# A planned attention and gated feed-forward kernel: other due times and other engines for its small jobs

## The chip, the core and the metric

The kernel runs on one core of a Trainium2 chip. TensorE (PE in the profile) multiplies matrices into PSUM; VectorE (DVE), ScalarE (ACT) and GpSimd (POOL) work on tiles in SBUF, and DVE and ACT on PSUM as well; SyncE (SP) issues the DMA transfers. The metric is the device time of one execution in microseconds (us); less is better.

## The reference

Eight batches of eight heads, 576 positions, 64 numbers a head. Queries and keys are rotated (rotary embedding), each head does a softmax attention, the heads of a batch are laid side by side to a 576x512 matrix `x`, and a gated feed-forward follows: a causal convolution of five taps gives the gate, and one matrix each stands before and after the gating.

```python
def rotate(x):
    x1, x2 = (x[..., :half], x[..., half:])
    return np.concatenate([x1 * cos - x2 * sin, x1 * sin + x2 * cos], axis=-1)
q_rot, k_rot = (rotate(q), rotate(k))
scores = scale * np.matmul(q_rot, k_rot.transpose(0, 1, 3, 2))
scores = scores - np.max(scores, axis=-1, keepdims=True)
attn = np.exp(scores)
attn = attn / (np.sum(attn, axis=-1, keepdims=True) + 1e-09)
x = np.matmul(attn, v)
...
for k in range(K):
    gate_pre += conv_w[k][None, None, :] * xp[:, k:k + S, :]
gate = 1.0 / (1.0 + np.exp(-gate_pre))
val = x @ w_val
return (gate * val @ w_out).astype(np.float32)
```

## The kernel before

Two heads make a pair, so there are 32 pairs, `p` = 0 to 31, and four pairs make a batch. The work is cut into 3445 jobs, most of them one instruction on one engine. For a pair they are:

- **Rotary steps**, for `k` and for `q`: two products with the tables (`rope_mul`, L212; keys `kmul0`, `kmul1`, `qmul0`, `qmul1`), their sum (`rope_add`, L216; `kadd`, `qadd`), a rounded high part on ACT (`qk_hi`, L223; `khi`, `qhi`) and the rest as a low part (`qk_lo`, L227; `klo`, `qlo`). `kadd` needs `kmul0` and `kmul1`; `klo` needs `khi`, which needs `kadd`.
- **Scores** on PE (`s_mm`, L255: five groups `s0` to `s4` a pair), the row maximum on DVE (`s_max`, L261), the exponential on ACT (`s_exp`, L274).
- **Turning the probabilities**: in pairs 5 to 30 four block transposes on DVE (`turn`, L289; `x1` to `x7`) and 16 moves by DMA (L294); in pairs 0 to 4 and in pair 31 by PE (L303, L316) with copies out of PSUM on ACT (L190) or DVE (L192), keys `c0` to `c7`.
- **Attention times values** on PE (`pv_last` L359, `pv_mm` L369 to L377), scaled on DVE into `x` (`x_norm`, L405; `norm0`, `norm1`). The sums of the softmax come by `chm`, a small copy on ACT (L190), and a trip through DRAM.
- **Gate**: tap 0 on ACT (L426), taps 1 to 4 on DVE (`tap`, L429), tanh on ACT (L433). `x_hi` (ACT, L412) and `x_lo` (POOL, L416; `xlo`) split `x` for the products.
- **Feed-forward**, for each batch 16 groups of 12 matmuls on PE (`f_mm`, L463): eight of the first stage (`f00` to `f07`), each followed by `y_mul` (DVE, L468), `y_hi` (ACT, L472) and `y_lo` (mostly POOL, L476), and eight of the second (`f10` to `f17`), each followed by a copy out and a DMA.

During pairs 0 to 4 DVE also decodes both weight matrices and the taps (L497 to L504).

What sets the order is `Plan`. Every job has a due time: a base that stands in the code, in a frame of 18.5 us a pair, plus an entry of the table `DUE`. `Plan.order` puts the jobs on one list: always the one with the smallest due time among those whose inputs and buffers are there. Each engine does its own jobs in the order of that list. `PICK` says for some jobs on which engine they go: `V` (DVE), `A` (ACT), `G` (POOL), `SP`. An entry without a suffix holds for pairs 5 to 31, with `e` for pairs 0 to 4 (rotary steps: 1 to 4), with `_0` and `_1` for the two halves of pair 0, with `l` for the last batch or pair.

DVE instructions that read two tensors of SBUF are marked as `port` jobs (rotary steps, taps 1 to 4, some decode steps). A POOL job that stands behind such a DVE job on the list is made to wait for the last one before it; nothing makes a DVE job wait for POOL:

```python
if jobs[i][6] and jobs[i][1] == "V":
    last = i
elif jobs[i][1] == "G" and last is not None:
    self.behind[i] = last
```

Of the kernel before, what the change touches and what calls it, by code (L numbers as in the profile page):

```python
# [35 lines left out]
PICK = {'c0': 'A', 'c0e': 'A', 'c1': 'V', 'c1e': 'V', 'c2': 'V', 'c2e': 'A', 'c3': 'A', 'c3e': 'A', 'c4': 'V', 'c4e': 'A', 'c5': 'A', 'c5e': 'A', 'c6': 'A', 'c6e': 'V', 'c7': 'V', 'c7e': 'A', 'ch0': 'A', 'ch0e': 'V', 'ch1': 'V', 'ch1e': 'A', 'chm': 'A', 'chme': 'A', 'cm': 'A', 'cme': 'A', 'kadd': 'G', 'kadd_0': 'V', 'kadd_1': 'V', 'kadde': 'V', 'kfront': 'A', 'kfronte': 'A', 'klo': 'G', 'klo_0': 'V', 'klo_1': 'V', 'kloe': 'G', 'kmul0': 'G', 'kmul0_0': 'V', 'kmul0_1': 'V', 'kmul0e': 'G', 'kmul1': 'V', 'kmul1_0': 'V', 'kmul1_1': 'V', 'kmul1e': 'V', 'od0': 'A', 'od0l': 'A', 'od1': 'A', 'od1l': 'V', 'od2': 'A', 'od2l': 'V', 'od3': 'A', 'od3l': 'A', 'qadd': 'G', 'qadd_0': 'V', 'qadd_1': 'V', 'qadde': 'V', 'qlo': 'G', 'qlo_0': 'G', 'qlo_1': 'G', 'qloe': 'G', 'qmixed': 'A', 'qmixede': 'A', 'qmul0': 'G', 'qmul0_0': 'V', 'qmul0_1': 'V', 'qmul0e': 'V', 'qmul1': 'G', 'qmul1_0': 'V', 'qmul1_1': 'V', 'qmul1e': 'V', 'xlo': 'G', 'xloe': 'G', 'xlol0': 'V', 'xlol1': 'G', 'ylo': 'G', 'ylol': 'V', 'ch3': 'V', 'ch3e': 'A', 'decout': 'A', 'decval': 'A', 'odma': 'SP', 'odmal': 'SP', 'loadk': 'SP', 'loadk_0': 'SP', 'loadk_1': 'SP', 'loadke': 'SP', 'loadq': 'SP', 'loadq_0': 'SP', 'loadq_1': 'SP', 'loadqe': 'SP', 'loadv': 'SP', 'loadve': 'SP', 'mv0': 'SP', 'mv1': 'SP', 'mv2': 'SP', 'mv3': 'SP', 'rr': 'SP', 'rre': 'SP', 'rw': 'SP', 'rwe': 'SP'}


class Plan:
# [769 lines left out]
```

## Time and profile before

| | |
|---|---|
| Median of 3 runs | 655.0 us (651.52 to 658.75) |
| The profiled execution | 652.48 us, span 650.7 us |
| DVE busy | 579.1 us (89%), 827 instructions |
| PE busy | 616.9 us (95%), 5683 matmuls |
| PE loading weights | 503.4 us (77%) |
| ACT busy | 462.7 us (71%), 1161 instructions |
| POOL busy | 390.3 us (60%), 297 instructions |
| Granted PE clock, mean | 0.996 |

A share over the whole span mixes three stretches: the head (pairs 0 to 4 with the weights), the steady stretch (pairs 6 to 30, in which a batch of four pairs repeats) and the tail (the last pair and the last batch's products). An instruction on DVE or POOL that waits for the SBUF port is counted as busy: its duration grows. So for these two, durations of equal instructions are compared with each other. The matmuls of PE overlap, so PE's busy share is read beside the time from the first of a group to the first of the next.

### The profile page before, as it was taken

What the parts mean: (1) busy time and instruction counts of PE and PEld (TensorE: products, weight loads), DVE (VectorE), ACT (ScalarE), POOL (GpSimd) and SP (SyncE); (2) the same over time, 40 slices, a digit from 0 to 9 for tenths busy, and PEclk for the clock granted to TensorE, in tenths of its full rate; (3) what the DMA queues carried; (4) which work ended last, traced back from release to release, by engine and by line L of the source; (5) the groups of instructions that cost most, each with busy time, mean ns of one, the idle gap of its engine ahead of it and who ended that gap; (6) DMA issues with size and microseconds to landing.
All of it is one profiled execution on the core that took longest, in us unless ns stands there. A gap on an engine that the chain in (4) does not pass through costs nothing.

```text
span 650.7 us, 15423 instructions
## 1 busy us (share of the span) xinstructions
PE 616.9 (95%) x5683; PEld 503.4 (77%) x5683; DVE 579.1 (89%) x827; ACT 462.7 (71%) x1161; POOL 390.3 (60%) x297
## 2 busy tenths in 40 slices
PE   8899988989899998999999999999999999999997
PEld 7666665678677886888778787888788877788797
DVE  6898999998899999999999999999999999995453
ACT  4788888867777777767877777767777777664521
POOL 1322446776777868687677868766976867630200
PEclk9899999999999999999999999999999999999999
DMA  5524432378989989999999999989999898864102
GB/s 185 225 78 153 162 117 101 114 206 242 268 235 260 258 250 250 263 241 252 239 249 252 241 262 255 267 241 256 254 263 254 233 252 210 249 166 132 56 2 74
DMA packets 51482, 134.43 MB, mean 207 GB/s; under 512 B 10928, under 2 KB 20944, under 8 KB 51408
## 3 DMA queue, kind: packets, MB, share of 16 engines
q1 hardware_dynamic: 50864, 132.86, 72.8%
q8 instruction: 45, 0.74, 0.5%
q10 hardware_dynamic: 544, 0.59, 0.3%
q14 instruction: 29, 0.24, 0.1%
HBM read 62.48 MB, written 9.59 MB: 111 GB/s over the span
## 4 chain that ended last, share of the span: by engine, by line
PE 49%; DVE 23%; DMA 9%; ACT 6%; issue 4%; POOL 4%; SPq 3%; ACTq 0%; DVEq 0%; POOLq 0%
PE ps_t L463 17%; PE ps_t L369 12%; PE ps_s L255 10%; DVE nm L261 8%; DVE big L289 7%; DMA big<-big 5%; DVE g L429 3%; SPq L294 3%; ACT p L274 3%; PE ps_t L359 3%; PE ps_t L303 2%; PE ps_t L374 2%; PE ps_t L330 1%; ACT big L190 1%; DVE g L468 1%
## 5 line engine op out<-in xcount | busy, mean ns | idle before, releaser
L261 DVE TENSOR_REDUCE nm<-ps_s 128x1 f32<-128x576 f32 x288 | 201.8, 741 | 19.9 <-PE ps_s L255 18.8
L274 ACT ACTIVATE p<-ps_s,nm 128x576 f32<-128x576 f32 x256 | 187.7, 738 | 39.5 <-DVE nm L261 38.4
L255 PE MATMUL ps_s<-k,q 64*128 64x288 f32 x1536 | 145.0, 310 | 11.4 <-ACT p L274 9.2
L255 PEld LDWEIGHTS ps_s<-k,q 64*128 64x128 f32 x1536 | 111.0, 184 | 37.6 <-ACT p L274 18.2
L289 DVE STREAM_TRANSPOSE big<-p 128x1152 f32<-128x1152 f32 x104 | 139.8, 1357 | 0.0
L429 DVE SCALAR_TENSOR_TENSOR g<-x,cw,g 128x576 f32<-128x576 f32 (+1 forms) x132 | 122.4, 927 | 0.9 <-ACT g L426 0.6
L369 PE MATMUL ps_t<-big,v 128*64 128x256 f32 (+2 forms) x1024 | 118.4, 382 | 0.0
L227 POOL TENSOR_TENSOR q<-iq,q 128x576 fp32r<-128x576 f32 (+2 forms) x33 | 48.8, 1477 | 94.9 <-ACT q L223 89.8
L369 PEld LDWEIGHTS ps_t<-big,v 128*64 128x64 f32 x1024 | 70.1, 137 | 44.1 <-issue 13.5
L212 POOL TENSOR_TENSOR iq<-iq,tab 128x576 f32<-128x576 f32 x54 | 77.1, 1450 | 19.8 <-DMA iq<-in_q 13.3
L463 PE MATMUL ps_t<-yh,wout_hi 128*128 128x288 f32 x256 | 79.2, 310 | 0.0
L463 PE MATMUL ps_t<-xh,wval_hi 128*128 128x288 f32 x256 | 79.0, 309 | 0.0
L463 PE MATMUL ps_t<-yl,wout_hi 128*128 128x288 f32 x256 | 76.2, 298 | 1.9 <-POOL yl L476 1.9
L463 PE MATMUL ps_t<-xl,wval_hi 128*128 128x288 f32 x256 | 76.3, 298 | 0.0
L463 PE MATMUL ps_t<-xh,wval_lo 128*128 128x288 f32 x256 | 75.9, 297 | 0.0
L463 PE MATMUL ps_t<-yh,wout_lo 128*128 128x288 f32 x256 | 75.5, 295 | 0.0
L227 POOL TENSOR_TENSOR k<-ik,k 128x576 fp32r<-128x576 f32 x31 | 52.5, 1694 | 37.4 <-DVE iq L212 25.0
L476 POOL TENSOR_TENSOR yl<-g,yh 128x288 fp32r<-128x288 f32 x56 | 46.7, 841 | 43.5 <-ACT yh L472 41.2
L416 POOL TENSOR_TENSOR xl<-x,xh 128x576 fp32r<-128x576 f32 (+1 forms) x32 | 47.6, 1487 | 25.5 <-PE ps_t L463 13.4
L463 PEld LDWEIGHTS ps_t<-xh,wval_hi 128*128 128x128 f32 x256 | 48.7, 190 | 2.8 <-issue 1.6
L472 ACT CAST yh<-g 128x288 fp32r<-128x288 f32 x64 | 26.6, 431 | 33.9 <-DVE g L468 33.9
L463 PEld LDWEIGHTS ps_t<-yl,wout_hi 128*128 128x128 f32 x256 | 48.3, 189 | 3.1 <-POOL yl L476 3.0
(95 smaller groups left out, 1107.9 us busy)
## 6 DMA issues: line engine op xcount, KB each, us to landing
big<-big SPq DMA_DIRECT2D x416, 144.0 KB
ik<-in_k SPq DMA_DIRECT2D x31, 576.0 KB
iq<-in_q SPq DMA_DIRECT2D x31, 576.0 KB
v<-in_v SPq DMA_DIRECT2D x32, 320.0 KB
rb<-rd SPq DMA_DIRECT2D x64, 144.0 KB
out_t<-oo SPq DMA_DIRECT2D x64, 144.0 KB
big<-in_w_val SPq DMA_DIRECT2D x4, 512.0 KB
big<-in_w_out SPq DMA_DIRECT2D x4, 512.0 KB
```

Of the source, the lines that this page charges most:

```text
L212: eng.tensor_tensor(out=t[:, i, a:b], in0=t[:, i, a:b], in1=tabs[:, i, a:b], op=ALU.mult)
L227: eng.tensor_tensor(out=t[:, 1], in0=state[p][n + "in"][:, 0, a:b], in1=t[:, 0].bitcast(F32), op=ALU.subtract)
L255: T.matmul(out=ps[:, half, 0:288], lhsT=st["q"][rows, x, c * 128:c * 128 + 128] if c < 4 else mixq[p % 2][:, x], rhs=st["k"][rows, y, k0:k ...
L261: V.tensor_reduce(out=st[f"nm{i}"], in_=st[f"s{i}"], axis=AX.XY, op=ALU.max, negate=True)
L274: A.activation(out=pd.rearrange("p (b x) -> p b x", b=2), in_=st[f"s{i}"], func=AF.Exp, bias=st[f"nm{i}"], scale=1.0, accum_out=sums[p % 2 ...
L289: V.transpose(out=t[:, :, cs.index(c)].rearrange("p b k i -> p k b i"), in_=st[f"p{c}"].rearrange("p h s -> p (h s)").rearrange("p (k b i) ...
L369: T.matmul(out=acc[HEAD[h], 0:n], lhsT=st["v"][:, j, h, :], rhs=st["pt"][:, :, c0:c1, 5 * place(p, 2 * c0 + h) + j].rearrange("p a c i -> ...
L416: eng.tensor_tensor(out=st["xl"][:, a:b], in0=xs[p % 2][:, 4 + a:4 + b], in1=st["xh"][:, a:b].bitcast(F32), op=ALU.subtract)
L429: V.scalar_tensor_tensor(out=g, in0=x_sb[:, a + k:b + k], scalar=w, in1=g, op0=ALU.mult, op1=ALU.add)
L463: T.matmul(out=acc[:, 0:n], lhsT=wt[w][:, kc, ds], rhs=mv, start=(kc == 0 and i == 0), stop=(kc == NCH - 1 and i == 2))
L472: A.copy(out=ffn[b, "h", dc, lo], in_=ffn[b, "y", dc, lo])
L476: eng.tensor_tensor(out=ffn[b, "l", dc, lo], in0=y, in1=ffn[b, "h", dc, lo].bitcast(F32), op=ALU.subtract)
```

## The change

Only the two tables differ, `DUE` and `PICK`. Not one job is added or taken away, and the code that makes the instructions is the same. All entries of `DUE` have new numbers; of those of `PICK` these have another engine:

```diff
-PICK = {'c0': 'A', 'c0e': 'A', 'c1': 'V', 'c1e': 'V', 'c2': 'V',
+PICK = {'c0': 'V', 'c0e': 'V', 'c1': 'A', 'c1e': 'A', 'c2': 'V',
...
-'c3': 'A', 'c4': 'V', 'c4e': 'A', 'c5': 'A', 'c6': 'A', 'c6e': 'V', 'c7': 'V',
+'c3': 'V', 'c4': 'A', 'c4e': 'V', 'c5': 'V', 'c6': 'V', 'c6e': 'A', 'c7': 'A',
...
-'ch1': 'V', 'kadd_1': 'V', 'qadd_1': 'V', 'qmul1_0': 'V', 'qmul1_1': 'V',
+'ch1': 'A', 'kadd_1': 'G', 'qadd_1': 'G', 'qmul1_0': 'G', 'qmul1_1': 'G',
...
-'kmul0e': 'G', 'kmul1e': 'V', 'qmul0e': 'V', 'qmul1e': 'V',
+'kmul0e': 'V', 'kmul1e': 'G', 'qmul0e': 'V', 'qmul1e': 'G',
...
-'od0l': 'A', 'od2l': 'V', 'xlol1': 'G',
+'od0l': 'V', 'od2l': 'A', 'xlol1': 'V',
```

In pairs 5 to 30 no job has another engine; there the change is one of order alone. DVE has seven jobs fewer (814 for 821), POOL seven more.

**On POOL, pairs 14 and 15** (the steady stretch; `iq`, `ik` are the rotary buffers, `yl` the low parts of the feed-forward). Before, from `qadd` of pair 15 on:

```order
L216 TENSOR_TENSOR iq_3544<-iq_3544 128x576
L227 TENSOR_TENSOR q_72<-iq_3544,q_72 128x576
L216 TENSOR_TENSOR ik_3412<-ik_3412 128x576
L212 TENSOR_TENSOR ik_3655<-ik_3655,tab 128x576
L227 TENSOR_TENSOR k_70<-ik_3412,k_70 128x576
L476 TENSOR_TENSOR yl_3851<-g_2768,yh_3850 128x288
```

And now:

```order
L216 TENSOR_TENSOR iq_3515<-iq_3515 128x576
L216 TENSOR_TENSOR ik_3377<-ik_3377 128x576
L227 TENSOR_TENSOR q_72<-iq_3515,q_72 128x576
L212 TENSOR_TENSOR ik_3621<-ik_3621,tab 128x576
L227 TENSOR_TENSOR k_70<-ik_3377,k_70 128x576
L476 TENSOR_TENSOR yl_3850<-g_2753,yh_3849 128x288
```

`kadd` (L216 on `ik`) stands ahead of `qlo` (L227 on `q`) instead of behind it. On the list it and `qlo` now come behind `kmul1` of DVE, which stands between taps 3 and 4; before, `qlo` came ahead of tap 3.

**On ACT at the same place**, from the exponentials of group `s1` on; before:

```order
L274 ACTIVATE p_3843,sums_86<-ps_s_3816,nm_3841 128x576
L274 ACTIVATE p_3843,sums_86<-ps_s_3817,nm_3845 128x576
L223 CAST k_70<-ik_3412 128x576
L190 COPY pq_3834<-ps_t_3886 128x512
L274 ACTIVATE p_3910,sums_86<-ps_s_3871,nm_3908 128x576
```

And now:

```order
L274 ACTIVATE p_3835,sums_86<-ps_s_3819,nm_3833 128x576
L274 ACTIVATE p_3835,sums_86<-ps_s_3820,nm_3837 128x576
L190 COPY pq_3840<-ps_t_3841 128x128
L223 CAST k_70<-ik_3377 128x576
L472 CAST yh_3849<-g_2753 128x288
```

The small copy `chm` (L190, 128x128) comes between the exponentials and `khi` (L223 on `k`), on which `klo` of POOL waits; before it stood ahead of the exponentials.

**On DVE in the head**, pair 3 coming up while pair 2 is scored (`ik_449` and `ik_498`, `iq_627`: rotary buffers; `big`: weights being decoded). Before, from `kmul1` on:

```order
L212 TENSOR_TENSOR ik_449<-ik_449,tab 128x576
L261 TENSOR_REDUCE nm_734<-ps_s_692 128x1
L503 TENSOR_SCALAR big_274<-big_274 128x512
L261 TENSOR_REDUCE nm_752<-ps_s_693 128x1
L429 SCALAR_TENSOR_TENSOR g_579<-x_84,cw,g_579 128x576
L216 TENSOR_TENSOR ik_449<-ik_449 128x576
L504 SCALAR_TENSOR_TENSOR wval_lo<-big_274 128x512
L212 TENSOR_TENSOR iq_627<-iq_627,tab 128x576
L429 SCALAR_TENSOR_TENSOR g_579<-x_84,cw,g_579 128x576
L212 TENSOR_TENSOR iq_627<-iq_627,tab 128x576
```

And now, from `kmul0` on:

```order
L212 TENSOR_TENSOR ik_498<-ik_498,tab 128x576
L216 TENSOR_TENSOR ik_498<-ik_498 128x576
L504 SCALAR_TENSOR_TENSOR wval_lo<-big_199 128x512
L429 SCALAR_TENSOR_TENSOR g_571<-x_84,cw,g_571 128x576
L261 TENSOR_REDUCE nm_777<-ps_s_697 128x1
L261 TENSOR_REDUCE nm_781<-ps_s_763 128x1
L405 TENSOR_TENSOR x_85<-ps_t_788,rb_723 128x320
L405 TENSOR_TENSOR x_85<-ps_t_787,rb_723 128x256
L261 TENSOR_REDUCE nm_870<-ps_s_764 128x1
L212 TENSOR_TENSOR iq_627<-iq_627,tab 128x576
L216 TENSOR_TENSOR iq_627<-iq_627 128x576
```

One of the two products of `q` has left DVE for POOL, and the other stands behind `norm0` and `norm1`.

## Rows read from the trace of the kernel before

**Rows 1.** By stretch: us; busy us of PE, PEld, DVE, ACT, POOL; clock; DMA share; GB/s.
```profile
5.00:135.00 130.00, 117.45 (x982) 84.71 (x980) 117.56 (x189) 100.61 (x245) 55.64 (x39) 0.99 0.40 139
150.90:575.00 424.10, 410.70 (x3952) 340.70 (x3949) 405.71 (x545) 316.88 (x806) 313.46 (x234) 1.00 0.92 249
575.00:651.00 76.00, 70.12 (x604) 61.74 (x603) 39.64 (x70) 31.00 (x76) 7.54 (x9) 0.99 0.27 76
```

**Rows 2.** Groups by line, shapes apart: busy us, mean ns; full taps, `y_lo` on POOL.
```profile
L429 DVE SCALAR_TENSOR_TENSOR g<-x,cw,g 128x576 f32<-128x576 f32 x124 | 118.3, 954 | 0.1
...
L476 POOL TENSOR_TENSOR yl<-g,yh 128x288 fp32r<-128x288 f32 x56 | 46.7, 841 | 43.5 <-ACT yh L472 41.2 <-DVE g L429 2.2
```

**Rows 3.** DVE in order of time: pairs 12 to 15, start us, us.
```profile
248.19 1.04 DVE L429 SCALAR_TENSOR_TENSOR g<-x,cw,g 128x576 f32<-128x576 f32 x1
...
256.38 1.26 DVE L429 SCALAR_TENSOR_TENSOR g<-x,cw,g 128x576 f32<-128x576 f32 x1
...
276.95 0.49 DVE L405 TENSOR_TENSOR x<-ps_t,rb 128x320 f32<-128x320 f32 x1 [0.52 <-PE ps_t L377]
277.93 1.42 DVE L261 TENSOR_REDUCE nm<-ps_s 128x1 f32<-128x576 f32 x2 [0.49 <-PE ps_s L255]
...
280.90 2.06 DVE L429 SCALAR_TENSOR_TENSOR g<-x,cw,g 128x576 f32<-128x576 f32 x1
...
293.62 0.92 DVE L429 SCALAR_TENSOR_TENSOR g<-x,cw,g 128x576 f32<-128x576 f32 x1
...
300.12 1.52 DVE L429 SCALAR_TENSOR_TENSOR g<-x,cw,g 128x576 f32<-128x576 f32 x1
```

**Rows 4.** POOL in order of time: pairs 14 and 15.
```profile
276.40 1.43 POOL L227 TENSOR_TENSOR q<-iq,q 128x576 fp32r<-128x576 f32 x1 [2.84 <-ACT q L223]
...
280.92 1.42 POOL L227 TENSOR_TENSOR k<-ik,k 128x576 fp32r<-128x576 f32 x1 [0.32 <-ACT k L223]
...
299.60 1.42 POOL L212 TENSOR_TENSOR ik<-ik,tab 128x576 f32<-128x576 f32 x1
```

**Rows 5.** ACT in order of time: `chm` and `khi` of pair 14.
```profile
278.19 0.27 ACT L190 COPY pq<-ps_t 128x128 f32<-128x128 f32 x1
...
280.17 0.67 ACT L223 CAST k<-ik 128x576 fp32r<-128x576 f32 x1
```

**Rows 6.** All engines in order of time: `qlo` beside tap 4 of pair 17's stretch.
```profile
328.14 1.80 DVE L429 SCALAR_TENSOR_TENSOR g<-x,cw,g 128x576 f32<-128x576 f32 x1
...
329.86 0.74 DVE L212 TENSOR_TENSOR ik<-ik,tab 128x576 f32<-128x576 f32 x1
330.53 0.80 DVE L429 SCALAR_TENSOR_TENSOR g<-x,cw,g 128x576 f32<-128x576 f32 x1
330.59 2.03 POOL L227 TENSOR_TENSOR q<-iq,q 128x576 fp32r<-128x576 f32 x1 [1.27 <-ACT q L223]
```

**Rows 7.** All engines in order of time: `qadd` between tap 3 and `kmul1`.
```profile
364.50 1.32 DVE L429 SCALAR_TENSOR_TENSOR g<-x,cw,g 128x576 f32<-128x576 f32 x1
...
365.16 1.93 POOL L216 TENSOR_TENSOR iq<-iq 128x576 f32<-128x576 f32 x1
...
365.74 1.97 DVE L212 TENSOR_TENSOR ik<-ik,tab 128x576 f32<-128x576 f32 x1
```

**Rows 8.** Busy time in the stretches of pairs 14 and 15, columns of rows 1.
```profile
273.10:292.80 19.70, 19.19 (x183) 16.34 (x181) 18.69 (x27) 13.89 (x36) 13.95 (x13) 1.00 0.95 253
292.80:310.20 17.40, 17.40 (x175) 14.49 (x173) 16.55 (x22) 12.62 (x34) 12.26 (x9) 1.00 0.92 259
```

**Rows 9.** Chain that ended last, tail: start us, us, what.
```profile
584.53 1.60 PE ps_t L463 x12
...
591.35 0.99 PE ps_s L255 x11
...
596.35 3.60 PE ps_t L369 x32
...
621.37 25.85 PE ps_t L463 x192
```

More of the change, by code (lines that the diff above doesn't have):

```diff
@@ L36 @@
-PICK = {'c0': 'A', 'c0e': 'A', 'c1': 'V', 'c1e': 'V', 'c2': 'V', 'c2e': 'A', 'c3': 'A', 'c3e': 'A', 'c4': 'V', 'c4e': 'A', 'c5': 'A', 'c5e': 'A', 'c6': 'A', 'c6e': 'V', 'c7': 'V', 'c7e': 'A', 'ch0': 'A', 'ch0e': 'V', 'ch1': 'V', 'ch1e': 'A', 'chm': 'A', 'chme': 'A', 'cm': 'A', 'cme': 'A', 'kadd': 'G', 'kadd_0': 'V', 'kadd_1': 'V', 'kadde': 'V', 'kfront': 'A', 'kfronte': 'A', 'klo': 'G', 'klo_0': 'V', 'klo_1': 'V', 'kloe': 'G', 'kmul0': 'G', 'kmul0_0': 'V', 'kmul0_1': 'V', 'kmul0e': 'G', 'kmul1': 'V', 'kmul1_0': 'V', 'kmul1_1': 'V', 'kmul1e': 'V', 'od0': 'A', 'od0l': 'A', 'od1': 'A', 'od1l': 'V', 'od2': 'A', 'od2l': 'V', 'od3': 'A', 'od3l': 'A', 'qadd': 'G', 'qadd_0': 'V', 'qadd_1': 'V', 'qadde': 'V', 'qlo': 'G', 'qlo_0': 'G', 'qlo_1': 'G', 'qloe': 'G', 'qmixed': 'A', 'qmixede': 'A', 'qmul0': 'G', 'qmul0_0': 'V', 'qmul0_1': 'V', 'qmul0e': 'V', 'qmul1': 'G', 'qmul1_0': 'V', 'qmul1_1': 'V', 'qmul1e': 'V', 'xlo': 'G', 'xloe': 'G', 'xlol0': 'V', 'xlol1': 'G', 'ylo': 'G', 'ylol': 'V', 'ch3': 'V', 'ch3e': 'A', 'decout': 'A', 'decval': 'A', 'odma': 'SP', 'odmal': 'SP', 'loadk': 'SP', 'loadk_0': 'SP', 'loadk_1': 'SP', 'loadke': 'SP', 'loadq': 'SP', 'loadq_0': 'SP', 'loadq_1': 'SP', 'loadqe': 'SP', 'loadv': 'SP', 'loadve': 'SP', 'mv0': 'SP', 'mv1': 'SP', 'mv2': 'SP', 'mv3': 'SP', 'rr': 'SP', 'rre': 'SP', 'rw': 'SP', 'rwe': 'SP'}
@@ new lines @@
+PICK = {'c0': 'V', 'c0e': 'V', 'c1': 'A', 'c1e': 'A', 'c2': 'V', 'c2e': 'A', 'c3': 'V', 'c3e': 'A', 'c4': 'A', 'c4e': 'V', 'c5': 'V', 'c5e': 'A', 'c6': 'V', 'c6e': 'A', 'c7': 'A', 'c7e': 'A', 'ch0': 'A', 'ch0e': 'V', 'ch1': 'A', 'ch1e': 'A', 'chm': 'A', 'chme': 'A', 'cm': 'A', 'cme': 'A', 'kadd': 'G', 'kadd_0': 'V', 'kadd_1': 'G', 'kadde': 'V', 'kfront': 'A', 'kfronte': 'A', 'klo': 'G', 'klo_0': 'V', 'klo_1': 'V', 'kloe': 'G', 'kmul0': 'G', 'kmul0_0': 'V', 'kmul0_1': 'V', 'kmul0e': 'V', 'kmul1': 'V', 'kmul1_0': 'V', 'kmul1_1': 'V', 'kmul1e': 'G', 'od0': 'A', 'od0l': 'V', 'od1': 'A', 'od1l': 'V', 'od2': 'A', 'od2l': 'A', 'od3': 'A', 'od3l': 'A', 'qadd': 'G', 'qadd_0': 'V', 'qadd_1': 'G', 'qadde': 'V', 'qlo': 'G', 'qlo_0': 'G', 'qlo_1': 'G', 'qloe': 'G', 'qmixed': 'A', 'qmixede': 'A', 'qmul0': 'G', 'qmul0_0': 'V', 'qmul0_1': 'V', 'qmul0e': 'V', 'qmul1': 'G', 'qmul1_0': 'G', 'qmul1_1': 'G', 'qmul1e': 'G', 'xlo': 'G', 'xloe': 'G', 'xlol0': 'V', 'xlol1': 'V', 'ylo': 'G', 'ylol': 'V', 'ch3': 'V', 'ch3e': 'A', 'decout': 'A', 'decval': 'A', 'odma': 'SP', 'odmal': 'SP', 'loadk': 'SP', 'loadk_0': 'SP', 'loadk_1': 'SP', 'loadke': 'SP', 'loadq': 'SP', 'loadq_0': 'SP', 'loadq_1': 'SP', 'loadqe': 'SP', 'loadv': 'SP', 'loadve': 'SP', 'mv0': 'SP', 'mv1': 'SP', 'mv2': 'SP', 'mv3': 'SP', 'rr': 'SP', 'rre': 'SP', 'rw': 'SP', 'rwe': 'SP'}
```

2 lines of the change are left out of this document (1 added, 1 removed).

## The prediction

> **What bounds the kernel now.** I read three things in this order: busy time by stretch, the durations of equal DVE instructions, and the order of time on DVE and POOL over one batch.
>
> By stretch [rows 1], DVE works 405.71 of the 424.10 us from 150.9 to 575 (96%), PE by its records 410.70, ACT and POOL three quarters. In the tail DVE falls to half and PE goes on. In the head DVE works 117.56 of 130 us and PE 117.45: two engines near their end, with waits between them. So time comes out of DVE, as long as PE can follow.
>
> DVE's busy time holds a wait. Undisturbed, a tap takes 0.80 us (330.53 in [rows 6]); the mean of the 124 full taps is 0.954 [rows 2]. So 124 x 0.154 = 19 us of DVE time is waiting inside taps. It is a hand-over with POOL: the tap of 2.06 us starts at 280.90 [rows 3], `klo` on POOL at 280.92 for 1.42 us [rows 4], and 1.42 + 0.7 is what the tap took. [Rows 6] show the other winner: tap 4 starts at 330.53 and keeps its 0.80, `qlo` starts 0.06 later and takes 2.03. [Rows 7] show the third case: `qadd` comes while tap 3 holds the port, waits, and then has it ahead of `kmul1`, which follows at once and takes 1.97 instead of 0.74 [rows 6].
>
> PE's floor: a feed-forward group takes 1.60 us [rows 9]. Pair 15's stretch has four, 6.4, and takes 17.4 with PE busy throughout [rows 8], so the rest of a pair (scores, 0.99 for each of the first four groups, attention with 3.60 for its main part, the turned rest [rows 9]) is at most 11.0. A batch has 16 groups: 4 x 11.0 + 25.6 = 69.6 us. It takes 71.8 (tap 3 of pair 13's stretch at 256.38, [rows 3], to that of pair 17's at 328.14, [rows 6]). PE allows a gain of some 2 us a batch.
>
> **Part 1, the steady stretch, pairs 6 to 30.** All engines keep their jobs, so only waits can change. I go through one batch; the five disturbed taps in [rows 3] lose 0.24 + 0.46 + 1.26 + 0.12 + 0.72 = 2.8 us against 0.80.
>
> *Pair 14's stretch.* POOL did `qlo`, `kadd`, `kmul0`, `klo` from 276.40 on, and `klo` met tap 1. Now `kadd` comes first, freed by `kmul1`'s end (about 275.3). Tap 4 starts at once behind `kmul1`, so `kadd` should wait for tap 4 as `qlo` did in [rows 6], then run 276.1 to 277.5, `qlo` to 278.9, `kmul0` to 280.3. `klo` still waits for `khi`, which ended at 280.84 [rows 5] and now has `chm` ahead of it (0.27 by its record, some 0.2 in a row of ACT instructions). So `klo` asks about 0.2 us after tap 1 has begun, tap 1 keeps 0.80, and 1.26 us are saved. But `klo` then runs 281.7 to 283.1, the first `y_lo` of the batch behind it to 283.9, and tap 2, now due near 283.3, waits about 0.55. Net -0.7.
>
> *Pair 15's stretch.* There `kmul0` (299.60 to 301.02, [rows 4]) held tap 1 for 0.72. With `kadd` first, and with both `y_lo` that stood in this chain moved ahead of tap 3, `kmul0` should end near the start of tap 1: I take 0.25 left. Net -0.5. The moved `y_lo` press on tap 3 and on `kmul1` (0.75 if one arrives as in [rows 7]); up to 1.0 us of such a delay is covered, since `norm1` and the next maximum wait 0.52 and 0.49 for PE behind this trio anyway [rows 3]. I cost it at nothing; uncovered it is up to +0.8 a batch.
>
> *Pair 12's stretch.* `klo` stands behind a `y_lo` now, and both end later; tap 2 waits about 0.5 instead of 0.24. Net +0.2.
>
> *Pair 13's stretch.* `qadd` ends about 0.5 later into tap 3; the same cover takes that. Net 0.
>
> Together -1.0 us a batch, times 6 batches: -6. Bounds: none saved and +0.8 from the trio, +5; all 2.8 saved, -17.
>
> At this place the Trainium skill ("SBUF — State Buffer", section "Who interferes with whom") says that whichever of the two engines issues first has the shared ports for its whole instruction, and the other fully blocks. The trace agrees for one pair of instructions, but not in full: the instruction at 280.90 issued first and lost to one 0.02 us later, and [rows 7] show that a waiting instruction comes ahead of the next in the other's row. By the rule alone `klo` would not have cost anything at 280.90, and the saving there would be nothing instead of 1.26.
>
> **Part 2, the head.** DVE loses eight rotary steps and gets one copy or so back elsewhere. Four are full products (`qmul1`, pairs 1 to 4), alike in size to `kmul1` with its 0.74, or 0.67 from its start to the next one's [rows 6]: -2.7 us. `kmul0` and `kmul1` change places between DVE and POOL, which cancels; the copies `c0`, `c4` replace `c1`, `c6` one for one. Against this stand four more POOL instructions of 1.4 us between DVE's port jobs. Each can cost DVE between 0 and the 1.26 of the worst tap: 0 to +5; I take 0.4 each, +1.6, since [rows 1] leave POOL over half idle here while DVE's port jobs are close together. The four halves in pair 0 go to POOL before anything else can run: two of them are ahead of the first scores and take about twice as long there, +0.4. Sum -0.7, bounds -4 and +6.
>
> **Part 3, the tail.** From 575 on PE works 70.12 of 76 us [rows 1], and the last 192 matmuls run without a gap, 25.85 us [rows 9]. Their number and pace stay. Three groups of the second stage now stand behind the last attention instead of ahead of it; 3 x 1.60 = 4.8 us of PE work cover the last `norm`, taps and splits. PE idles at most 5.9 us there, mostly at the very end behind the last product. I take 0, bounds -2 and +2.
>
> **Sum.** -6 - 0.7 + 0 = -6.7 us on the profiled execution's 652.48: 645.8. That execution lies 2.5 us under the median of the runs, and a median is what will be compared, so 655.0 - 6.7 = 648.3, rounded to 648.5.
>
> **Rivals.**
> *A: nothing comes of it.* The port is nearly full: a pair has five DVE port jobs (3.7 us) and on POOL eight of 1.42 [rows 4] and two of 0.84 [rows 2], 13.0 us; together 16.7 of the 17.8 that a pair takes on average. What is pushed off tap 1 meets tap 2, tap 3 or the trio, and PE waits cover less than I think. For it: in three of my four stretches something comes back. Against: the two largest waits have one named cause each. Time: part 1 between 0 and +5, 654 to 660, say 656.
> *B: much more comes.* Every tap keeps 0.80 and the trio's waits shrink too; PE sets the pace at 69.6 us a batch, -2.2 x 6 = -13, and the head gives -3: 637 to 643, say 639. Against it: PE is busy throughout in pair 15's stretch [rows 8]. The skill ("Perfetto Trace Analysis", section "Identifying the Most-Contended Engine") would judge PE's room by its weight loads instead, 340.70 of 424.10 us or 80% [rows 1], and so find 20% room, which would leave DVE's own floor: 71.8 less the 2.8 of the taps and about 3 of waits for PE, 66 a batch, and 655 - 6 x 5.8 = 620 us. The pace of the groups in the chain [rows 9] speaks against that here, and I give it no more than the upper end of B.
> *C: slower, at tap 4.* `kadd` is now freed by `kmul1`, with tap 4 directly behind it. If POOL's request gets the port before tap 4 does, tap 4 loses 1.2 to 1.4 us in each of some 25 pairs, as the tap at 280.90 did. The waits of `norm1` and of the next maximum hide up to 1.0 of it, so 0.3 to 0.9 a pair is left: +8 to +22 on top of what else is gained, 655 to 672, say 664. It decides between a request 0.02 us behind the start of a tap (lost, at 280.90) and one 0.06 behind it (kept, [rows 6]). `kadd` cannot ask before `kmul1` has ended, and tap 4 starts 0.07 before that (330.53 against 329.86 + 0.74, [rows 6]); so I hold it unlikely.
> That the order does not change is excluded: it stands different on all engines.
>
> **How the numbers follow.** Forecast 0.45, A 0.27, B 0.11, C 0.17. About 1% (6.5 us) is what a measurement of this kernel can tell from no change. The forecast spans 643 to 654 and lies about half on either side of 648.5, B is faster, A the same. Faster: 0.23 + 0.11 = 0.34. Slower: C's upper two thirds and the worst of A (all bounds of parts 1 and 2 together), 0.18. The same: 0.48. The range leaves out most of B below 640 and C above 663: 640 to 663.
>
> **What would show it.** Right: in the changed profile the mean of the full taps falls from 0.954 to about 0.90, tap 1 keeps 0.80 in pair 14's kind of stretch with `klo` starting behind its end or with a long record beside it, and tap 2 grows there; batches take near 70.5 us; DVE has four long products fewer in the head, and it ends 0 to 3 us earlier. Rival C: tap 4 near 2.0 us in most pairs. Rival A: the mean of the taps as before, with the long ones at other places. I am wrong altogether if a queue that I left alone decides, above all SP's: loads, moves and the trip of the sums stand in another order there, and a late one would show as waits for DMA on PE or on `norm0`; the rows shown here name none.

## The result, and the profile after

The changed kernel took 646.36 us (median of 4 executions, 644.88 to 647.28) against 656.48 us of the kernel before on the same chip (651.52 to 658.75): ratio 0.985 [0.981, 0.990] (95% interval). Timed again later (6 executions against 23), it was 0.986 [0.982, 0.991], that is 8.9 us less [6.2, 11.7]; the medians of these executions, 648.23 and 655.30 us, lie 7.1 apart. The ratios, here and below, leave out the few executions that took over 1.5% longer than the fastest of their kernel. The forecast was -6.7 us. The two profiled executions lie exactly 6.7 apart (652.48 and 645.8), and chance has a part in that: second profiles of the two programs took 652.29 and 648.21. So below I give both profiles of each.

By stretch, columns as in [rows 1], the changed kernel's first profile (the limits moved with the end of the head):

```profile
5.00:135.00 130.00, 116.22 (x1001) 85.21 (x1000) 120.62 (x186) 105.52 (x254) 67.38 (x48) 1.00 0.42 140
144.00:568.00 424.00, 413.58 (x3995) 342.68 (x3995) 400.84 (x551) 319.11 (x814) 321.85 (x238) 1.00 0.92 252
568.00:644.00 76.00, 70.43 (x611) 62.31 (x609) 40.17 (x71) 30.58 (x76) 6.63 (x7) 1.00 0.28 79
```

In the steady stretch DVE's busy time fell from 405.71 to 400.84 of 424 us while PE's rose from 410.70 to 413.58 [rows 1]: DVE loses less in waits, PE does more per time. In the head DVE is busier than before (120.62 against 117.56), although it has less to do there; POOL took 67.38 instead of 55.64. The groups that answer [rows 2]:

```profile
L429 DVE SCALAR_TENSOR_TENSOR g<-x,cw,g 128x576 f32<-128x576 f32 x124 | 113.3, 914 | 0.1
...
L476 POOL TENSOR_TENSOR yl<-g,yh 128x288 fp32r<-128x288 f32 x56 | 46.8, 835 | 46.4 <-ACT yh L472 42.6 <-DVE g L429 3.8
```

The mean of the full taps fell from 954 to 914 ns (970 and 883 in the second profiles). Pair 14's stretch, DVE in order of time, answers the first half of [rows 3]:

```profile
272.26 0.81 DVE L429 SCALAR_TENSOR_TENSOR g<-x,cw,g 128x576 f32<-128x576 f32 x1
272.99 0.98 DVE L405 TENSOR_TENSOR x<-ps_t,rb 128x256 f32<-128x256 f32 x2
274.46 1.42 DVE L261 TENSOR_REDUCE nm<-ps_s 128x1 f32<-128x576 f32 x2 [0.49 <-PE ps_s L255]
...
277.42 0.80 DVE L429 SCALAR_TENSOR_TENSOR g<-x,cw,g 128x576 f32<-128x576 f32 x1
...
279.89 1.01 DVE L429 SCALAR_TENSOR_TENSOR g<-x,cw,g 128x576 f32<-128x576 f32 x1
```

And POOL beside it, which answers [rows 4]:

```profile
272.42 1.93 POOL L216 TENSOR_TENSOR ik<-ik 128x576 f32<-128x576 f32 x1 [2.01 <-DVE ik L212]
274.32 1.44 POOL L227 TENSOR_TENSOR q<-iq,q 128x576 fp32r<-128x576 f32 x1
275.69 1.45 POOL L212 TENSOR_TENSOR ik<-ik,tab 128x576 f32<-128x576 f32 x1
277.61 1.91 POOL L227 TENSOR_TENSOR k<-ik,k 128x576 fp32r<-128x576 f32 x1 [0.46 <-ACT k L223]
279.48 0.81 POOL L476 TENSOR_TENSOR yl<-g,yh 128x288 fp32r<-128x288 f32 x1
```

Read the two side by side. `kadd` (272.42) asks 0.16 behind the start of tap 4 (272.26), tap 4 keeps its 0.81, and the wait is inside `kadd`'s record, 1.93 instead of 1.42. `klo` (277.61) asks 0.19 behind tap 1 (277.42): tap 1 takes 0.80 instead of 2.06, `klo` 1.91. Tap 2 (279.89) then pays 0.2 for the `y_lo` that ends at 280.29. In pair 15's stretch `kmul0` on POOL now ends at 295.72, beside a tap 1 that starts at 295.65 and takes 0.78 (it took 1.52):

```profile
294.30 1.42 POOL L212 TENSOR_TENSOR ik<-ik,tab 128x576 f32<-128x576 f32 x1
```

On ACT, `chm` stands directly ahead of `khi` (compare [rows 5], where it came before the two exponentials) and takes 0.14 to `khi`'s start:

```profile
276.70 0.26 ACT L190 COPY pq<-ps_t 128x128 f32<-128x128 f32 x1
276.84 0.69 ACT L223 CAST k<-ik 128x576 fp32r<-128x576 f32 x1
```

The chain that ended last [rows 9] still ends in PE's matmuls without a gap, 228 in a row at 0.134 us each (it was 192 at 0.135):

```profile
606.05 3.60 PE ps_t L369 x32
610.24 30.52 PE ps_t L463 x228
```

Where the time went is read from the starts of the reciprocals of the softmax sums, one for each pair and counted from 0 like the pairs: "the sixth" is that of pair 6. Pair 4's starts at 108.6 and 107.9 us before, at 107.8 and 107.9 after; pair 8's at 186.9 and 186.2, then at 184.2 and 184.3. The 20 pairs from there take 355.5 and 357.0, then 353.5 and 355.4; the two pairs behind them 37.9 and 36.8, then 35.6 and 36.0; from pair 30's to the end it is 70.4 and 70.5, then 70.7 and 70.7. So -0.4 by pair 4, -1.9 from there to pair 8, -1.8 in the 20 steady pairs, -1.5 in two more, +0.25 in the tail: -5.4 between the means of two profiles. The ratio says -8.9; both profiles of before lie some 2.5 us under 654.9, the median of 80 executions of it timed beside the experiments.

### The profile page after: what moved, and what is told of

Read it like the earlier page. It is cut to its first block, busy times and chain, and to the rows that moved or that the text cites. A ratio compares the mean times of both kernels' runs of the same rounds, so it can differ in the third digit from the quotient of the medians.

```text
span 644.0 us, 15384 instructions
## 1 busy us (share of the span) xinstructions
PE 612.9 (95%) x5683; PEld 502.1 (78%) x5683; DVE 569.8 (88%) x820; ACT 463.7 (72%) x1161; POOL 404.6 (63%) x304
## 4 chain that ended last, share of the span: by engine, by line
PE 73%; DVE 13%; DMA 4%; ACT 4%; POOL 2%; issue 2%; SPq 1%; DVEq 0%; POOLq 0%; ACTq 0%
PE ps_t L463 29%; PE ps_s L255 17%; PE ps_t L369 17%; DVE nm L261 5%; PE ps_t L359 3%; DVE g L429 3%; DVE big L289 2%; PE ps_t L374 2%; PE ps_t L330 2%; ACT p L274 2%; DMA big<-big 2%; PE ps_t L303 1%; POOL xl L416 1%; DMA rb<-rd 1%; PE ps_t L345 1%
## 5 line engine op out<-in xcount | busy, mean ns | idle before, releaser
L255 PE MATMUL ps_s<-k,q 64*128 64x288 f32 x1536 | 144.1, 311 | 11.7 <-ACT p L274 9.6
L429 DVE SCALAR_TENSOR_TENSOR g<-x,cw,g 128x576 f32<-128x576 f32 (+1 forms) x132 | 117.3, 890 | 1.8 <-ACT g L426 1.5
L212 POOL TENSOR_TENSOR iq<-iq,tab 128x576 f32<-128x576 f32 (+2 forms) x60 | 84.6, 1428 | 35.7 <-DMA iq<-in_q 25.7
L216 POOL TENSOR_TENSOR ik<-ik 128x576 f32<-128x576 f32 (+1 forms) x28 | 50.5, 1804 | 45.9 <-DVE ik L212 44.0
L227 POOL TENSOR_TENSOR k<-ik,k 128x576 fp32r<-128x576 f32 x31 | 49.7, 1603 | 35.3 <-ACT k L223 35.1
L416 POOL TENSOR_TENSOR xl<-x,xh 128x576 fp32r<-128x576 f32 x31 | 47.7, 1538 | 20.2 <-ACT xh L412 18.3
L274 ACT ACTIVATION_READ_ACCUMULATOR p<-ps_s,nm 128x1 f32 x256 | 50.7, 198 | 0.0
L463 PEld LDWEIGHTS ps_t<-yh,wout_hi 128*128 128x128 f32 x256 | 48.9, 191 | 2.2 <-PE ps_s L255 1.8
```

The costliest lines, as they stand in the source:

```text
L212: eng.tensor_tensor(out=t[:, i, a:b], in0=t[:, i, a:b], in1=tabs[:, i, a:b], op=ALU.mult)
L216: eng.tensor_tensor(out=t[:, 0], in0=t[:, 0], in1=t[:, 1], op=ALU.add)
L227: eng.tensor_tensor(out=t[:, 1], in0=state[p][n + "in"][:, 0, a:b], in1=t[:, 0].bitcast(F32), op=ALU.subtract)
L255: T.matmul(out=ps[:, half, 0:288], lhsT=st["q"][rows, x, c * 128:c * 128 + 128] if c < 4 else mixq[p % 2][:, x], rhs=st["k"][rows, y, k0:k ...
L274: A.activation(out=pd.rearrange("p (b x) -> p b x", b=2), in_=st[f"s{i}"], func=AF.Exp, bias=st[f"nm{i}"], scale=1.0, accum_out=sums[p % 2 ...
L416: eng.tensor_tensor(out=st["xl"][:, a:b], in0=xs[p % 2][:, 4 + a:4 + b], in1=st["xh"][:, a:b].bitcast(F32), op=ALU.subtract)
```

## The experiments

My theory: the steady stretch gains because `kadd` goes ahead of `qlo` on POOL and `khi` comes later on ACT, so that neither `klo` nor `kmul0` takes the port from tap 1. Rival 1: the gain comes out of the head, where alone engines changed. Rival 2: ACT's order carries it, POOL's does nothing. Rival 3: `kadd` ahead of `qlo` is all of it. All ratios are against the kernel before on the same chip.

**One half of the table each.** The new due times and engines for the head's keys alone, the rest as before; and the reverse.

```diff
 # kernel before, for the head's keys (…_0, …_1, …e, warm, tables, weights, taps)
-DUE[key], PICK[key] of before
+DUE[key], PICK[key] of the changed kernel
```

> The kernel before with the due times and engines of the head alone (pair 0, the front of pair 1, and all keys that end in e), so the steady stretch and the tail keep their old order. My theory: the head is worth 1 to 2 us, so about -1.5 us against before (ratio 0.995 to 1.000), the batches from the sixth reciprocal to the 30th take 429.4 us as before, and the full taps keep their long ones at tap 1. Rival 1, the gain comes out of the head, where alone engines were changed: -5 to -8 us, ratio 0.988 to 0.992.

> The changed kernel with the head's due times and engines of before: steady stretch and tail alone. My theory: -5 to -5.5 us against before (ratio about 0.992), the 24 pairs between the sixth and the 30th reciprocal in 423.5 to 424.5 us, the head's end as before at about 150.9. Rival 1 (the head carries it): 0 to -1 us.

Measured: the new head alone 673.88 us, ratio 1.030 [1.026, 1.034], 19 us slower; the new steady stretch alone 653.1 us, 0.997 [0.994, 1.000]. Neither theory had this. In the first kernel the loss stands between the reciprocals of pairs 3 and 5 (92.6 and 152.9; 91.2 and 134.8 before), where this is PE's longest wait:

```profile
122.08 1.33 PE L255 MATMUL ps_s<-k,q 64*128 64x288 f32 x8 [4.15 <-ACT p L274]
```

That is a group of pair 5's scores waiting for an exponential. My reading of it, which no run tests by itself: the jobs of pair 4 are planned by the head's keys, those of pair 5 by the steady ones, and the two sets no longer fit. In the second kernel the same seam costs 4.2 us (sixth reciprocal 153.7, changed kernel 149.4 and 149.5); from there its 24 pairs take 426.6, the changed kernel's 423.9 and 426.2. So its steady part ran as in the changed kernel, and the halves cannot be priced by taking them apart at this seam.

**`kadd` ahead of `qlo` alone.** One due time; 27 places on POOL, no other engine's order.

```diff
-'qlo': -22.751
+'qlo': 8.45
```

> The kernel before with one due time changed, that of qlo: on POOL kadd, freed by kmul1, now stands ahead of qlo in pairs 5 to 31, as in the changed kernel; every other engine keeps the order of before. My theory: tap 1 in pair 15's kind of stretch (299.60 to 301.02 for kmul0 in rows 4) loses its 0.72 us, since kmul0 ends at its start or before; but klo still meets tap 1 at its start in pair 14's kind (khi has nothing ahead of it on ACT), and tap 1 stays at about 2.06 there. So -0.5 us a batch, -3 us in all (ratio 0.995), and tap 4 keeps 0.80. Rival 2, the order on ACT carries the gain and POOL's does nothing: 0 us. Rival 3, kadd before qlo is the whole of the steady gain: -5 to -6 us, with tap 1 at 0.80 in both kinds.

Measured: 656.13 us, 1.0036 [1.0012, 1.0061], slower by 0.8 to 4.0 us. All three expectations fell. Pair 15's kind did get better (tap 1 1.37 in the mean instead of 1.55 and 1.44), but pair 16's kind, whose tap 1 had taken 0.92 to 1.02, now takes 2.05 to 2.06 in every batch:

```profile
318.52 2.05 DVE L429 SCALAR_TENSOR_TENSOR g<-x,cw,g 128x576 f32<-128x576 f32 x1
```
```profile
316.95 1.44 POOL L212 TENSOR_TENSOR ik<-ik,tab 128x576 f32<-128x576 f32 x1
318.54 1.42 POOL L227 TENSOR_TENSOR k<-ik,k 128x576 fp32r<-128x576 f32 x1 [0.15 <-ACT k L223]
```

In the kernel before, the same three were these:

```profile
317.43 0.92 DVE L429 SCALAR_TENSOR_TENSOR g<-x,cw,g 128x576 f32<-128x576 f32 x1
```
```profile
316.30 1.44 POOL L212 TENSOR_TENSOR ik<-ik,tab 128x576 f32<-128x576 f32 x1
317.69 1.94 POOL L227 TENSOR_TENSOR k<-ik,k 128x576 fp32r<-128x576 f32 x1
```

There `kmul0` ended 0.31 behind the start of tap 1 and `klo` had to stand behind it, asking 0.26 late. With `kadd` first, `kmul0` ends ahead of the tap, `klo` waits for `khi` alone, and asks 0.02 behind the tap's start. So here a POOL queue that is earlier makes its next instruction meet the tap.

**`chm` back to its place.** The changed kernel, ACT's order alone.

```diff
-'chm': 5.7539, 'exp2': -29.6743, 'exp3': -19.2531
+'chm': -2.5032, 'exp2': 16.6, 'exp3': 16.1
```

> The changed kernel with three due times changed (chm, exp2, exp3), so that on ACT alone chm goes back to its place of before, khi has nothing ahead of it, and klo on POOL can ask some 0.2 us earlier. My theory: klo then asks within some 0.03 us of tap 1's start in pair 14's kind of stretch, gets the port, and tap 1 takes about 2.06 instead of 0.80, once a batch; tap 2 gets 0.2 back. +0.7 to +1.0 us a batch, +4 to +6 us against the changed kernel, so -3 to -5 against before (ratio about 0.993 to 0.996). Rival 2, kadd before qlo alone carries the gain and 0.2 us of klo don't matter: no difference from the changed kernel, about -9 us against before, tap 1 at 0.80.

Measured: 653.44 us, 0.998 [0.996, 1.001]; against the changed kernel's 0.986 that is +7.8 us. Tap 1 takes 2.05 to 2.06 in pair 14's kind in five batches of six, and `klo` asks 0.02 behind it:

```profile
281.43 2.06 DVE L429 SCALAR_TENSOR_TENSOR g<-x,cw,g 128x576 f32<-128x576 f32 x1
```
```profile
281.45 1.43 POOL L227 TENSOR_TENSOR k<-ik,k 128x576 fp32r<-128x576 f32 x1 [0.31 <-ACT k L223]
```

Rival 3 falls: without `chm`, `kadd` ahead of `qlo` is worth next to nothing. The place was as I said, and the time shows at it: from the reciprocals of pairs 9, 13, 17, 21 and 25 to the next, the stretches with this tap 1, it is 19.2 to 20.4 us, in the two profiles of the changed kernel 18.3 to 18.7. The price was more than I expected: tap 1 of pair 15's kind went to 1.40 as well (0.82 and 0.78 in the changed kernel).

**`chm` alone, and both.** The kernel before with one due time, then with two.

```diff
-'chm': -2.5032
+'chm': 23.6
```
```diff
-'chm': -2.5032, 'qlo': -22.751
+'chm': 23.6, 'qlo': 8.45
```

> The kernel before with one due time changed, that of chm: on ACT alone chm now stands behind exp2 and exp3, directly ahead of khi (with f14, where there is one), as in the changed kernel; POOL, DVE, PE and SP keep the order of before. My theory, as the runs so far leave it: klo asks some 0.2 us after tap 1's start in pair 14's kind of stretch, tap 1 keeps 0.80 there instead of 2.06, tap 2 pays 0.5 of it back; pair 15's kind stays at 1.5. Net -0.7 a batch, -4 us, ratio 0.993 to 0.995. Rival: the delay of klo pays only with kadd ahead of qlo (POOL else runs later throughout): 0 us, with the loss at tap 2 or tap 3 instead.

> The kernel before with both due times changed, chm's and qlo's: kadd ahead of qlo on POOL, and chm directly ahead of khi on ACT. My theory: both parts together give what the steady stretch gained in the changed kernel, -5 to -6 us (ratio 0.991 to 0.992), though kadd ahead of qlo alone gave +2. Rival: the two add up, -4 + 2 = -2 us; then what else changed (qmixed later and qadd earlier, vz earlier, the y_lo moved) has a part in the gain.

Measured: `chm` alone 653.32 us, 0.9964 [0.9934, 0.9995], 2.4 us less [0.3, 4.3]; both 651.34 us, 0.991 [0.988, 0.994], 5.8 us less [3.7, 7.9] (the medians of these two, 651.34 and 655.30, lie 4.0 apart). With `kadd` alone at +2.4, the two would add up to nothing; together they give -5.8. Rival 2 falls with it: ACT's order alone gives less than half. The rows of the taps fit. With `chm` moved, tap 1 of pair 14's kind keeps 0.80 in all its stretches from pair 10 to 30, `klo` asking 0.18 late:

```profile
281.92 0.80 DVE L429 SCALAR_TENSOR_TENSOR g<-x,cw,g 128x576 f32<-128x576 f32 x1
```
```profile
282.10 1.91 POOL L227 TENSOR_TENSOR k<-ik,k 128x576 fp32r<-128x576 f32 x1 [0.44 <-ACT k L223]
```

but pair 15's kind stays at 1.54. With both, pair 15's comes to 1.12 and pair 16's to 0.80, where `klo` now asks 0.18 to 0.19 late. So by the ratios, 27 instructions moved on POOL and 26 on ACT make up some two thirds of the gain, and their effect on tap 1 is shown.

The one profile of this kernel (652.96 us) does not show the time coming back, though. Its full taps take 913 ns in the mean, as in the changed kernel's first profile (914), yet the 24 pairs from pair 6 to 30 take 432.0 us, more than in either profile of before (429.4 and 429.8). In these pairs DVE waits 3.2 us for the DMA of the softmax sums ahead of `x_norm` (1.6 and 2.2 in the profiles of before, 0.7 and 0.2 in those of the changed kernel). PE waits 2.3 us, by the profile for a DMA of keys (0.8 and 0.7 before, never in the changed kernel). The kernel with `chm` put back is the counterpart: 0.2 us for the sums and nothing for keys, but the long tap 1, and 429.5 us (`chm` alone: 427.5). Of these four kernels only the changed one, which has both the short taps and the prompt transfers, is faster in this stretch by its traces. Whether the order on SP's queue, which changed too, has a part in the gain was not tried. The rest (`qmixed`, `vz`, `qadd`, the moved `y_lo`) was not taken apart either.

**The changed kernel again, and the kernel before again.**

> The changed kernel once more, with more timed runs, for a tighter interval and a second profile. Between the two profiles of before and after lay 6.7 us, between the medians of four runs each 10.1. My theory (the sum of the prediction): 6 to 8 us faster than before. If the head or the clock's dips (3.4 us at the lower level, one in each of the two profiles) carried the rest: 9 to 11.

> The kernel before once more, for a second profile of it: how far one profile of the same program lies from another, by stretch, and whether its long taps stand at the same places. My theory: tap 1 near 2.06 in most of pair 14's kind and near 1.5 in pair 15's, batches of 71 to 72 us, the total between 652 and 658.

Measured: 648.23 us, 0.986 [0.982, 0.991], -8.9 us: above the 6 to 8 of the sum, below the 9 to 11 of the alternative, and the interval holds both. The second profile of before took 652.29 us, as expected, but it has the long tap 1 in pair 14's kind in two of five batches (0.84 and 0.80 in two others, where `klo` asked 0.18 late), the first in three of five.

**The four `qmul1` back on DVE.** The changed kernel, four instructions on another engine.

```diff
-'qmul1e': 'G'
+'qmul1e': 'V'
```

> The changed kernel with one engine changed: the four qmul1 of pairs 1 to 4 back on DVE, all else in the same order. By the prediction's part 2: +2.7 us for four products of 0.67 on DVE, -1.6 for four POOL instructions fewer, so +1.1 us against the changed kernel. Rival: the head's long DVE steps in the changed kernel (taps of 1.55 to 2.08 in pairs 0 to 3) come from these POOL instructions, each of which holds the port for 1.4 us or pushes others onto the taps: -2 to -5 us against the changed kernel. Second rival: DVE's work is covered in the head, no difference.

Measured: 648.24 us, 0.988 [0.984, 0.992], no difference from the changed kernel, the second rival's number. The sixth reciprocal stands at 149.5 in both. DVE's busy time in the head is about equal as well:

```profile
5.00:135.00 130.00, 117.17 (x1001) 86.15 (x1000) 120.52 (x191) 105.97 (x255) 63.89 (x44) 0.99 0.43 143
```

120.52 with the four products, 120.62 and 119.54 without them in the two profiles of the changed kernel: of their 2.7 us, 1.7 to 2.8 came back in port waits. The long DVE port steps of the head lie 11.1 and 10.1 us over the time of their undisturbed like in those two profiles and 7.5 here (counted from 0.1 us above the lower quartile of equal steps), that is 0.6 to 0.9 us for each of the four POOL instructions and not 0.4.

**`cm` behind `exp5`, once a batch.** The changed kernel, six swaps on ACT.

```diff
-at("cm" + ph, t + 18.2, ...
+at("cm" + ph, t + 18.2 + 35.1 * (p % 4 == 3 and p >= EARLY), ...
```

> The changed kernel with cm, the eviction of tm on ACT, behind exp5 instead of ahead of it, in one stretch of each batch (pairs 8, 12, 16, 20, 24, 28): there exp5 waited on ACT behind cm, cm for PE, and then PE's third score group 1.08 us for exp5 (at 315.4 in the changed kernel's trace); the dips of the clock in the changed kernel's second profile begin within some 2 us of this gap. If PE bounds the steady stretch as the prediction has it (69.6 of 70.7 us a batch): the gap goes from the rows, so do the dips behind it, DVE's waits for PE shrink, and 0.5 to 1.1 us a batch come back, -3 to -7 us against the changed kernel, some 12 to 16 us (ratio 0.976 to 0.982) against before. Rival: DVE bounds it, which runs without a gap at this place; the time stays within 1 us of the changed kernel's, and the gap on PE comes back elsewhere.

Measured: 648.5 us, 0.992 [0.988, 0.995], no better than the changed kernel. The wait went, and another came behind the scores in the same stretch. First the changed kernel (pair 16's stretch), then this one (pair 12's):

```profile
316.50 1.06 PE L255 MATMUL ps_s<-k,q 64*128 64x288 f32 x11 [1.08 <-ACT p L274]
```
```profile
250.85 0.40 PE L463 MATMUL ps_t<-yl,wout_hi 128*128 128x288 f32 x1 [1.17 <-POOL yl L476]
```

The scores come earlier, and the second-stage group behind them waits 1.17 us for a `y_lo`, where it waited 0.36 in the changed kernel. The rival had it half: the gap comes back, though for POOL's sake.

**The heads exchanged up to pair 2.** A last attempt to price the head, with the seam between pairs 2 and 3.

```diff
-plan.add(base + DUE.get(key, 0.0), e, ...
+plan.add(base + (OLD.get(key, DUE.get(key, 0.0)) if p < 3 else DUE.get(key, 0.0)), e, ...
```

> The changed kernel with the due times and engines of before for the head's keys in pairs 0 to 2 (and the tables and weights that are planned with them); from pair 3 on those of the changed kernel, and from pair 6 on its very order. Unlike the kernel with the whole old head, the seam lies between pairs planned alike. Profiles of the two kernels stand 0.3 us apart at the fourth reciprocal (107.9 and 108.6 against 107.8 and 107.9) and 2.2 at the eighth (186.2, 186.9 against 184.2, 184.3). My theory: the head's own order is worth nothing, the gain by the eighth pair is the same as the steady one and begins with pair 5, so this runs as the changed kernel does, -8 to -9 us against before (ratio about 0.987). If the head carries 2 us or more: ratio 0.990 to 0.993.

> The reverse: the kernel before with the head's due times and engines of the changed kernel for pairs 0 to 2, and those of before from pair 3 on. My theory: 0 us against before (ratio 0.998 to 1.002); if the head carries 2 us or more, 0.994 to 0.997; if a seam costs by itself as in the two kernels with the heads exchanged whole, over 1.003 here and in the reverse alike.

Measured: 666.55 us, 1.018 [1.013, 1.023], and 666.92 us, 1.018 [1.013, 1.023]: the third outcome. Both are 12 us slower than before, whichever head stands ahead of the seam; for the first, made from the changed kernel, that is some 20 us over the kernel that it came from. In its trace the sixth reciprocal stands at 167.4 (149.4 in the changed kernel), in the other's at 160.0 (150.9 before). In the first the longest waits of PE from 60 to 160 us are these (what it waited for, us, times, longest):

```profile
PE ps_t L307 <- ACT p L278: 5.7, 3, 2.0
PE ps_t L543 <- ACT wout_hi L538: 4.2, 2, 3.0
```

PE waits for exponentials and weight casts of ACT there. I take it that they stand in an order which the other head's DVE does not serve in time; no run shows that by itself. What the head alone is worth stays open.

## Why the prediction was right

**What bounds.** Right, and it shows in where the gain stopped. In the second profile DVE's busy time is 396.16 of 424 us, 9 to 12 less than in like stretches of the two profiles of before (405.61 and 407.76), and PE's 415.11. The time of the 24 pairs from pair 6 on fell by less, since DVE then waits for PE: 16 and 13 us before, 21 and 27 in the changed kernel. The row of its second profile:

```profile
144.00:568.00 424.00, 415.11 (x3977) 345.54 (x3977) 396.16 (x547) 318.50 (x811) 318.95 (x236) 0.98 0.93 252
```

Rival B needed every tap at 0.80 and batches of 69.6 us. In the second profile the taps come near it (883 ns), yet the batches take 71.1 us; four of them hold a fall of PE's clock (last section). In the kernel with the old head up to pair 2, whose order is the changed kernel's from pair 8 on and whose trace has no such fall there, the five batches from pair 8 to 28 take 69.9 us in the mean. So PE's floor is borne out within 0.3 us, but the other four traces in this order stay above it, at 70.7 to 71.2.

**Pair 14's stretch.** The mechanism holds step by step: `kadd` waits behind tap 4 at no loss, `klo` asks 0.19 late, tap 1 keeps 0.80, tap 2 pays. The sizes were off both ways. I put -1.26 in every batch, but the collision stood in three of five batches of one profile and two of five of the other, so tap 1 fell by 0.75 in the mean (1.67 and 1.43 to 0.80); tap 2 pays 0.2 and not 0.55, as the first `y_lo` ended earlier than I had it. That the sum came out near is thus partly luck: here the saving and what is paid back were both put too high, and pair 12's kind, below, has the other sign.

**Pair 15's.** -0.5 forecast, -0.7 measured (1.55 and 1.44 to 0.82 and 0.78): `kmul0` ends 0.07 into the tap, I had left 0.25. **Pair 12's** was wrong in sign: +0.2 forecast; taps 1 and 2 of that kind came from 0.95 and 1.04 to 0.80 and 0.81. `klo` does stand behind a `y_lo` there, but ends only 0.1 into tap 2 (314.44 + 1.40 against 315.74), which loses nothing by it, and tap 1 no longer meets `kmul0`. **Pair 13's:** the trio costs nothing, as said; tap 4 keeps 0.81 and `kmul1` 0.74.

**The sum of part 1.** -6 forecast over 24 pairs; between the profiles the 24 pairs behind the sixth reciprocal took 429.4 and 429.8 before, 423.9 and 426.2 after: -4.6. Kernels whose order is the same as one of the two from pair 8 on give the spread: 355.5, 357.0, 358.1 and 360.1 us for the 20 pairs in before's order, 349.3, 353.5, 355.4, 355.6 and 355.8 in the new one, means 357.7 and 353.9, -0.8 a batch for the -1.0 forecast.

**Part 2.** -0.7 for the head; by pair 4 it is -0.4, by pair 8 -2.3, most of it behind pair 4, where the steady mechanism begins: the first tap of pairs 4 to 6 fell from 0.94, 1.27 and 1.26 to 0.79, 0.78 and 0.99, and a `kmul1` of 1.97 in pair 5 to 0.74. The single terms were mis-sized where I had chosen a value between bounds: 0.4 for each POOL instruction was 0.6 to 0.9, which eats the whole 2.7 or nearly. Pairs 5 to 8 I had counted with neither part in full.

**Part 3.** 0 forecast, +0.25 measured, the last matmuls at the same pace.

**Rival C** (POOL wins at tap 4) is refuted in all steady pairs: tap 4 is 0.81 and `kadd` 1.92 to 1.95. Its deciding point can now be given closer. In the traces of before, its repetition and the experiments with `kadd` and `chm`, `klo` asked 0.015 to 0.021 us behind the start of tap 1 sixteen times between pairs 10 and 26, and tap 1 took 2.05 or 2.06 each time; requests 0.054 us or more behind it never had the port: where such a tap took over 0.83, an earlier POOL instruction was still in it. In seven traces the last full tap is met by a POOL instruction 0.029 to 0.034 us behind its start, and takes 2.06 to 2.08. So in these rows the boundary lies between 0.034 and 0.054 us. One case in the head does not fit: in the kernel with `cm` moved, a POOL product that starts 0.02 ahead of a tap takes 2.05, and the tap keeps 0.75. The Trainium skill ("SBUF — State Buffer", section "Who interferes with whom") has it that whoever issues first holds the port; by that rule, and by the starts in the records, none of the sixteen would have lost. It holds from 0.054 us on; for less, this case's rows decide.

**Rival A** fell by the interval. What stays open: how much of the 8.9 us is the head's, how much is that of the queues not tried alone, SP's above all, and why the ratio says more than the profiles (-5.4).

## What to carry to other kernels

Where two engines share a port, look for a coincidence that repeats: `klo` hung on the last exponential of a group and tap 1 on the turn beside it, so they could meet within 0.02 us in one batch after another, and a small copy of 0.14 us put back to its old place in one queue cost 7.8 us of the 8.9, where four jobs moved to another engine changed nothing. Price such edits together: `kadd` earlier was +2.4 us alone, `chm` later -2.4, both -5.8. And do not price half of a tuned order by grafting it onto another: three of four grafts came out 12 to 19 us slower than the kernel before and said nothing of the halves.

## What the runs showed of the hardware that was not expected

PE's clock leaves its upper level (2.4 GHz) for the lower (1.2 GHz) for 3.4 us at a time, now and then for twice that, and where it does so differs between executions of one program. In the changed kernel's second profile it did so in four batches, each time within 4 us behind the start of the once-a-batch wait of 1.08 us; in the first profile not once at that place. The kernel with `qmul1` back on DVE, of the same order there, has them at the same four places. One of them, in windows of 4 us with the clock third from the end:

```profile
386.00:390.00 4.00, 2.92 (x25) 2.36 (x23) 3.79 (x6) 3.58 (x10) 4.00 (x4) 1.00 1.01 299
390.00:394.00 4.00, 3.65 (x16) 3.38 (x14) 3.61 (x4) 2.64 (x8) 4.00 (x4) 0.57 0.88 240
394.00:398.00 4.00, 4.00 (x44) 2.62 (x44) 3.54 (x6) 2.95 (x9) 2.07 (x2) 1.00 0.91 246
```

PE had idled from 387.36 to 388.44 and again 0.35 us before 390.57, and the window of 4 us at the lower level counts 16 matmuls, the next one 44. What a dip costs can be read in the rows. In the five traces whose order is the changed kernel's from pair 8 on, the stretch from the reciprocal of pair 11, 15, 19, 23 or 27 to the next takes 18.9 to 19.1 us in the ten cases that hold a dip and 18.0 to 18.3 in the fifteen that hold none: 1.0 us more, and mostly some 0.3 in the stretch behind it.

The times agree. Over the 80 executions of the kernel before, those with a mean granted clock of 0.994 or more took 653.6 us in the mean, those under 0.9895 took 657.0. A regression of time on clock gives 3.7 us for 0.01, so about 1.0 us for one such dip (3.4 us at half the pace are 0.0026 of the span). The changed kernel's ten executions have a mean clock of 0.9934 against 0.9913, which by this line would be 0.8 of the 8.9 us; which of the two, waits or clock, causes the other, the line does not say.
